# One weight load of 128 rows issued as seven loads of 8, 8, 8, 8, 8, 8 and 80 rows

## The chip, the core and the metric

The kernel runs on one core of a Trainium2 chip. The metric is the device time of one execution in microseconds (us), as the median over runs; lower is better. The trace of one profiled execution shows five engines: PE (matrix multiplication, with PEld for its weight loads), DVE (vector work), ACT (activations and copies), POOL (small vector work) and SP, which does nothing in this kernel but issue DMA transfers. The transfers themselves run on the core's 16 DMA engines.

## What is computed

Three layers in a row, all in float32: a windowed attention, a soft mixture of eight experts, and a gated feed-forward layer.

```
scores = scale * np.matmul(q, k.transpose(0, 1, 3, 2))      # masked to a window, softmax, then @ v
...
slot_input = slot_input.reshape(E, S_per_e, D)              # E = 8 experts, 4 slots each
for e in range(E):
    h = np.maximum(slot_input[e] @ w1[e], 0.0)
    slot_out[e] = h @ w2[e]
...
h = x @ w_in
g = h * (1.0 / (1.0 + np.exp(-h)))
return (g @ w_out).astype(np.float32)
```

The change concerns how one sixteenth of the experts' second weight matrix, `w2`, is brought from memory.

## The kernel before

The attention runs over 16 pairs of heads until about 96 us. While it runs, SP already brings in the experts' weights: `w1` in 16 pieces and `w2` in 16 pieces, each a tile of 128 rows by 2048 numbers (1 MB). Then PE runs the expert layer: L1.0 to L1.15 multiply by the pieces of `w1`, and L2.0 to L2.15 by the pieces of `w2`, one group of matmuls for each piece. In the listing `l1(i)` and `l2(i)` are these groups, `load_w1(i)` and `load_w2(i)` the loads. After the last of them come the weights of the third layer, `w_in` (tiles `wi0`, `wi1`, ...) and `w_out` (tiles `wo0`, ...). They arrive as 64-bit numbers and DVE converts them with three operations each (`conv`, lines 634, 636 and 638: the groups `cvi` for `w_in` and `cvo` for `w_out`). `wi0` and `wo0` come as two halves of 512 KB each. From about 134 us on PE multiplies without a break until the end.

What is issued when:

- All loads are issued by SP from one list, in one fixed order: ... `w2.7`, `w2.8`, `w2.9` to `w2.13`, the two halves of `wo0`, the first half of `wi0`, `w2.14`, `w2.15` in three parts, the second half of `wi0`, `wi1`, `wo1` and so on. SP handles one issue after the other; what waits there holds back all behind it.
- From `w2.8` on a piece of `w2` is loaded into a place that held a piece of `w1`, so its issue waits until PE has multiplied by that piece: `w2.8` waits for L1.1, `w2.9` for L1.2, up to `w2.13` for L1.6. The halves of `wo0` go where `w1.14` was, so they wait for L1.14.
- The framework gives each load, in the order of issue, one of eight semaphores in turn (`DMAHW0` to `DMAHW7` in the order listings). A load is issued only when the load that had the same semaphore before, eight places earlier in the list, has landed in full. At most eight loads are under way.
- The order on the engines in this part of the program is written out by hand (`LATER`, from line 1270); on DVE the conversions come in the order `hr1` (line 550, the last step of L1), `cvo` of the first half of `wo0`, and so on, to the conversion of the second half of `wi0`, after which PE makes its first operand of the third layer.

Two lines say how the operation that the change touches is put in the list:

```
   577	    for i in range(16):
   580	            op(f"lw2.{i}", "SP", 2.46, d, lambda i=i: load_w2(i))
```

Of the kernel before, what the change touches and what calls it, by code (L numbers as in the profile page):

```python
# [23 lines left out]
DFF = 2048  # L24
NT = B * S
EPS = 1e-9
XW = 129
JH = 6
CBANK = ((2, 1), (5, 1), (4, 6), (5, 1))
# [3 lines left out]
def fused_kernel(ctx: ExitStack, tc: tile.TileContext, a: dict):  # L33
    nc = tc.nc
    pe, act, dve, pool, sp = nc.tensor, nc.scalar, nc.vector, nc.gpsimd, nc.sync
# [20 lines left out]
    gmx = cp.tile([128, 1], F32, name="gmx")  # L56
    acc = cp.tile([128, XW], F32, name="acc")
    mrun = cp.tile([128, 2], F32, name="mrun")
# [16 lines left out]
    def new(place, key, dt=F32):  # L75
        tiles[key] = cp.tile([128, SIZE[place]], dt, tag=place, name=f"{place}_{key}")
        return tiles[key]

    def reg(key, off, n):
        return tiles[key][:, off:off + n]  # L80
# [4 lines left out]
    def mm(out, lhsT, rhs, start, stop):  # L85
        pe.matmul(out, lhsT=lhsT, rhs=rhs, start=start, stop=stop, skip_group_check=True)  # L86
# [11 lines left out]
    def op(name, eng, cost, deps, fn):  # L98
        kind = name.rstrip("0123456789.")
        if kind in INORDER and kind in last:  # L100
            deps = deps + [last[kind]]
        last[kind] = name
        ops[name] = (eng, cost, [d for d in deps if d], fn)
# [47 lines left out]
    def xreg(n):  # L151
        return reg("xb", (n % 5) * 5 * XW, 5 * XW).rearrange("p (t c) -> p t c", t=5)

# [88 lines left out]
    def recip(n, j0=0, j1=NJ):  # L242
        r, rows = n % 2, slice(j0 // 3, j1 // 3)
        dve.tensor_scalar(out=sume[:, r, rows], in0=sums[:, r, j0:j1].rearrange("p (a b) -> p a b", b=3), scalar1=EPS, scalar2=None, op0=ALU.add)  # L244
        dve.reciprocal(out=rinv[:, r, j0:j1].rearrange("p (a b) -> p a b", b=3), in_=sume[:, r, rows])  # L245
# [155 lines left out]
    def dc(b):  # L401
        for t in range(5):
            m = rows(t)
            for g in range(4):
                mm(mb[32 * g:32 * g + 32, 192:192 + XW], le[0:m, t, :], xreg(4 * b + g)[0:m, t, :], t == 0, t == 4)

# [4 lines left out]
    def ca4(b):  # L411
        dve.tensor_reduce(out=csm, in_=cn, axis=AXX, op=ALU.add)
        dve.tensor_scalar(out=csm, in0=csm, scalar1=EPS, scalar2=None, op0=ALU.add)  # L413
        dve.reciprocal(out=csm, in_=csm)
# [31 lines left out]
    for b in range(B):  # L446
# [4 lines left out]
            out=gmx, in_=lb[:, 0:160], axis=AXX, op=ALU.max))  # L451
# [12 lines left out]
        if b:  # L464
            op(f"dwe{b}", "ACT", .3, [f"dw{b}", f"ds{pb}"], lambda b=b: act.activation(out=wgt, in_=mrun, func=ACTF.Exp, bias=t4[:, 1:2]))
            op(f"dacc{b}", "DVE", .55, [f"dwe{b}"], lambda b=b: dacc(b))
            op(f"ds{b}", "DVE", .35, [f"dc{b}", f"dacc{b}"], lambda b=b: dve.scalar_tensor_tensor(
                out=acc, in0=mb[:, 192:192 + XW], scalar=wgt[:, 1:2], in1=acc, op0=ALU.mult, op1=ALU.add))
        else:
            op(f"ds{b}", "DVE", .2, [f"dc{b}"], lambda b=b: dve.tensor_copy(acc, mb[:, 192:192 + XW]))  # L470
        op(f"caa{b}", "DVE", .32, las + [f"cab{pb}" if b else f"pt{NPAIR-4}.3", "sie" if b == B - 1 else None],
# [29 lines left out]
    def fz():  # L501
        dve.tensor_scalar(out=t4[:, 2:3], in0=acc[:, 128:129], scalar1=EPS, scalar2=None, op0=ALU.add)
        dve.reciprocal(out=t4[:, 2:3], in_=t4[:, 2:3])
# [29 lines left out]

    def load_w2(i, g0=0, g1=4):
        t = new(W2S[i], f"w2.{i}") if g0 == 0 else tiles[f"w2.{i}"]
        sp.dma_start(out=t[:, 512 * g0:512 * g1], in_=a["w2"][i, :, 512 * g0:512 * g1])

    def l1(i):
        h, e = divmod(i, 8)
# [37 lines left out]
    for i in range(16):  # L577
        d = free2.get(W2S[i], []) + ([f"L1.{i-7}"] if i >= 8 else [])
        if i < 15:
            op(f"lw2.{i}", "SP", 2.46, d, lambda i=i: load_w2(i))  # L580
        else:
            for k, n in enumerate(("lw2.15", "lw2b", "lw2c")):
                op(n, "SP", .00482 * (W2C[k + 1] - W2C[k]), d, lambda k=k: load_w2(15, W2C[k] // 128, W2C[k + 1] // 128))
        d = [f"lw2.{max(i, L2W)}", f"hr{i//8}", f"te{N1}", f"L2.{i-1}" if i else None]
        if i < 15:
            op(f"L2.{i}", "PE", .86, d, lambda i=i: l2(i))
        else:
            op("L2a", "PE", .46, d, lambda: l2(15, 0))
            op("L2b", "PE", .24, ["L2a", "lw2b"], lambda: l2(15, 1))
            op("L2.15", "PE", .34, ["L2b", "lw2c"], lambda: l2(15, 2))  # L590
# [243 lines left out]
    for f in (0, 1, *range(2, 16, 2)):  # L834
        i = f // 2
# [213 lines left out]
    for c in range(NC):  # L1049
# [17 lines left out]
        for j in range(4):  # L1067
            r = lambda b: [f"cs{c}.{'ABCE'.index(b)}.{i}" for i in (2 * j, 2 * j + 1)]
# [5 lines left out]
        for g, p in enumerate(SEQ):  # L1074
            for j in range(4):
# [3 lines left out]
                r = lambda b: [f"cs{c}.{'ABCE'.index(b)}.{i}" for i in (2 * j, 2 * j + 1)]  # L1079
# [4 lines left out]
            for i in range(8):  # L1084
# [3 lines left out]
                for y in (6, 7) if i > 5 else (i,):  # L1088
                    d += [f"sh{c}.{p}.{y//2}", f"sl{c}.{p}.{y//2}"]
                    t = 3 if k == 4 else k  # L1090
# [431 lines left out]
```

## Time and profile before

| what | us |
|---|---|
| median of 3 runs | 344.35 (343.3 to 344.42) |
| the profiled execution | 343.64 |
| its span, first to last instruction | 341.5 |
| PE busy | 329.4 (96% of the span) |
| DVE busy | 263.3 (77%) |
| ACT busy | 221.9 (65%) |
| DMA: bytes moved | 70.03 MB, mean 205 GB/s |

The profiled execution is 2.1 us longer than its span: what lies before the first and behind the last instruction. Its slices of time (40 of 8.5 us each) show the DMA engines full and moving 400 to 420 GB/s from 8 us to 136 us, and nearly idle after 150 us. The granted TensorE clock is full speed in every slice. The rows below come from six views: the chain of waits (the work that ended last, followed back), the busy time by stretch, the issues in order of time on SP, the list of transfers with the time from issue to landing, the waits of SP's queue, and the instructions of DVE and PE in order of time.

### The profile page before, as it was taken

The page shows a single profiled execution, that of the slowest core. Times are in us where ns is not written, and L with a number is a line of the kernel's source. Part 1 is how long each engine was busy: PE and PEld are TensorE (multiplying, and loading weights), DVE is VectorE, ACT ScalarE, POOL GpSimd, SP SyncE. Part 2 cuts the span into 40 slices and gives each one's busy share as a digit, 9 for nine tenths or more (in the row PEclk, how much of TensorE's full clock was granted, in tenths as well). Part 3 has the DMA queues.
Part 4 walks back from the last instruction along what each step waited for, and adds up shares of the span by engine and source line. Part 5 has one row for each costly group of instructions (what it writes and reads, how often), then busy time and mean ns, then how long its engine had stood idle before and what let it go on. Part 6 is the DMA issues. An engine that isn't in the chain of part 4 may idle for free.

```text
span 341.5 us, 8179 instructions
## 1 busy us (share of the span) xinstructions
PE 329.4 (96%) x3221; PEld 272.1 (80%) x3232; DVE 263.3 (77%) x479; ACT 221.9 (65%) x639; POOL 74.6 (22%) x121
## 2 busy tenths in 40 slices
PE   7998999999899999999999999999999999999995
PEld 3687877777633337788888888999999999999995
DVE  5777877689660099999999997989994654999573
ACT  3599989797430125778496999996467666645540
POOL 6987978675260000000000000000000000000000
PEclk9999999999999999999999999999999999999999
DMA  7999999999999999818390000110200011000004
GB/s 259 405 405 406 403 401 407 416 404 415 416 405 423 416 411 419 349 58 322 125 356 15 0 0 2 55 68 2 77 3 0 0 71 69 3 23 23 2 22 147
DMA packets 17893, 70.03 MB, mean 205 GB/s; under 512 B 1984, under 2 KB 4288, under 8 KB 12096
## 3 DMA queue, kind: packets, MB, share of 16 engines
q1 hardware_dynamic: 17856, 69.53, 51.9%
q8 instruction: 25, 0.41, 0.5%
q14 instruction: 12, 0.10, 0.1%
HBM read 64.80 MB, written 4.72 MB: 204 GB/s over the span
## 4 chain that ended last, share of the span: by engine, by line
PE 83%; DMA 8%; DVE 3%; ACT 2%; POOL 1%; issue 1%; DVEq 0%; ACTq 0%; POOLq 0%
PE ps L86 80%; DMA w_w2.13_1760<-in_w 5%; PE ps L312 3%; DMA w_wi<-in_w_in 3%; ACT rt_px L232 1%; DMA rs_raw<-in_q 1%; POOL rv_v L1138 1%; ACT rt_px L301 1%; POOL rb_a L180 0%; PE ps L434 0%; POOL ra_a L180 0%; ACT x_xb L315 0%; DVE stats L227 0%; DVE csm L413 0%; DVE spaced L244 0%
## 5 line engine op out<-in xcount | busy, mean ns | idle before, releaser
L1083 DVE TENSOR_TENSOR rt_stl<-w_raww,rs_sth 128x768 fp32r<-128x768 f32 (+1 forms) x52 | 42.2, 830 | 18.2 <-ACT rs_sth L1081 17.9
L86 PE MATMUL ps<-w_ws,x_gz 128*128 128x512 f32 x216 | 53.6, 393 | 0.0
L86 PE MATMUL ps<-rs_sth,w_ws 128*128 128x384 f32 x192 | 53.1, 334 | 0.0
L1081 ACT CAST rs_sth<-w_raww 128x768 fp32r<-128x768 f32 (+1 forms) x52 | 37.8, 738 | 22.3 <-PE ps L86 16.6
L232 ACT ACTIVATE rt_px<-ps,spaced 128x64 f32<-128x64 f32 x144 | 43.5, 332 | 10.2 <-DVE spaced L228 8.5
L86 PEld LDWEIGHTS ps<-w_ws,x_gz 128*128 128x128 f32 x216 | 40.0, 188 | 7.7 <-issue 0.4
L86 PEld LDWEIGHTS ps<-rs_sth,w_ws 128*128 128x128 f32 x192 | 35.1, 188 | 0.0
L232 ACT ACTIVATION_READ_ACCUMULATOR rt_px<-ps,spaced 128x1 f32 x144 | 32.3, 225 | 0.0
L86 PE MATMUL ps<-rt_stl,w_ws 128*128 128x384 f32 x96 | 32.1, 334 | 0.0
L86 PE MATMUL ps<-ct_ct,rv_astk 128*128 128x384 f32 x96 | 27.3, 338 | 0.0
L1066 ACT ACTIVATE w_raww<-ps 128x384 f32<-128x384 f32 x48 | 22.0, 493 | 7.1 <-PE ps L86 7.0
L249 POOL TENSOR_TENSOR rt_px<-rt_px,stats 128x576 f32<-128x576 f32 (+2 forms) x17 | 18.6, 1093 | 8.2 <-DVE stats L245 3.4
L86 PEld LDWEIGHTS ps<-ct_ct,rv_astk 128*128 128x128 f32 x96 | 17.6, 188 | 2.4 <-issue 0.4
L86 PEld LDWEIGHTS ps<-rt_stl,w_ws 128*128 128x128 f32 x96 | 18.0, 188 | 0.0
L896 ACT ACTIVATE x_gz<-ps 128x768 fp32r<-128x768 f32 (+3 forms) x18 | 13.3, 740 | 4.8 <-PE ps L86 4.7
L899 DVE TENSOR_TENSOR x_gz<-rt_gtm,x_gz 128x768 fp32r<-128x768 f32 (+3 forms) x18 | 15.5, 864 | 1.0 <-ACT rt_gtm L889 0.9
L1081 ACT CAST rs_sth<-x_rawx 128x768 fp32r<-128x768 f32 x12 | 10.0, 837 | 9.6 <-PE ps L86 6.3
L889 ACT ACTIVATE rt_gtm<-ps 128x768 f32<-128x768 f32 (+3 forms) x18 | 13.2, 742 | 3.8 <-PE ps L86 3.6
L86 PEld LDWEIGHTS ps<-ra_a,rv_v 128*64 128x64 f32 x320 | 13.3, 137 | 2.8 <-issue 1.1
L86 PE MATMUL ps<-ra_a,rv_v 128*64 128x96 f32 (+2 forms) x320 | 14.9, 241 | 0.4 <-DVE ra_a L263 0.3
L1083 DVE TENSOR_TENSOR rt_stl<-x_rawx,rs_sth 128x768 fp32r<-128x768 f32 x12 | 11.5, 954 | 4.7 <-ACT rs_sth L1081 4.6
L315 ACT COPY x_xb<-ps 128x640 f32<-128x640 f32 x16 | 11.3, 708 | 5.7 <-PE ps L312 3.5
(298 smaller groups left out, 772.2 us busy)
## 6 DMA issues: line engine op xcount, KB each, us to landing
w_wi<-in_w_in SPq DMA_DIRECT2D x7, 1024.0 KB, 7.1
rs_wo<-in_w_out SPq DMA_DIRECT2D x4, 1024.0 KB, 5.8
rk_k<-in_k SPq DMA_DIRECT2D x12, 288.0 KB, 7.6
w_wo<-in_w_out SPq DMA_DIRECT2D x3, 1024.0 KB, 4.7
rs_raw<-in_v SPq DMA_DIRECT2D x9, 288.0 KB, 9.4
rs_raw<-in_q SPq DMA_DIRECT2D x8, 288.0 KB, 6.5
w_more<-in_q SPq DMA_DIRECT2D x8, 288.0 KB, 9.4
w_more<-in_v SPq DMA_DIRECT2D x6, 288.0 KB, 8.0
```

The source lines that it names most:

```text
L86: pe.matmul(out, lhsT=lhsT, rhs=rhs, start=start, stop=stop, skip_group_check=True)
L232: act.activation(out=preg(n)[:, j, :], in_=sj(n, j), func=ACTF.Exp, scale=D ** -0.5, bias=nmx[:, r, j // 3, j % 3:j % 3 + 1], accum_out=su ...
L249: pool.tensor_tensor(out=p, in0=p, in1=rinv[:, n % 2, j0:j1].rearrange("p (j o) -> p j o", o=1).to_broadcast([128, j1 - j0, 64]), op=ALU.mult)
L301: act.copy(out=x, in_=src)
L312: pe.transpose(ps[0:m, c:c + 128], x[:, 128 * t:128 * t + m], ident)
L315: act.copy(out=xreg(n)[:, :, 0:128], in_=ps[:, TC:TC + 640].rearrange("p (t c) -> p t c", c=128))
L889: act.activation(out=cols(gt(f), x), in_=hbs(x), func=ACTF.Silu)
L896: act.activation(out=cols(gbuf(f, 0), x), in_=hbs(x), func=ACTF.Silu)
L899: dve.tensor_tensor(out=gsl(gbuf(f, 1), x), in0=gsl(gt(f), x), in1=gsl(gbuf(f, 0), x), op=ALU.subtract)
L1066: op(f"cs{x}", "ACT", .385, [f"ch{x}", *d], lambda c=c, b=b, i=i, s=s: act.activation(out=at(c, b, i), in_=bank[6 + s][:, 0:TW], func=ACTF ...
L1081: op(f"sh{x}", "ACT", cost(c, PRODS[p][0], j, .42, .74), [*src, old, "cvo14" if o < 0 else None], lambda c=c, p=p, j=j: both(c, p, j, 0, l ...
L1083: lambda c=c, p=p, j=j: both(c, p, j, 1, lambda x, h, l: dve.tensor_tensor(out=l, in0=x, in1=h, op=ALU.subtract)))
```

## The change

`load_w2` issues one transfer for a piece of `w2`, rows 0 to 128. With the change, piece 8 alone is issued as seven transfers: rows 0 to 8, 8 to 16, and so on to 40 to 48, and then rows 48 to 128. All seven write into the same tile, from the same place in memory, and together they move the same 1 MB.

```
+EIGHTS = [(r, r + 8) for r in range(0, 48, 8)] + [(48, 128)]
...
     def load_w2(i, g0=0, g1=4):
         t = new(W2S[i], f"w2.{i}") if g0 == 0 else tiles[f"w2.{i}"]
-        sp.dma_start(out=t[:, 512 * g0:512 * g1], in_=a["w2"][i, :, 512 * g0:512 * g1])
+        for r0, r1 in EIGHTS if i == 8 else ((0, 128),):
+            sp.dma_start(out=t[r0:r1, 512 * g0:512 * g1], in_=a["w2"][i, r0:r1, 512 * g0:512 * g1])
```

No instruction of PE, DVE, ACT or POOL changes its place. On SP the list grows by six rows, and the semaphores in brackets move with it. In the listings `w_w2.8_1683` is the tile of piece 8, the brackets hold what the issue waits for, and `PE_49` is PE's own semaphore. SP around piece 8, before:

```order
L536 DMA rv_w2.6_1634<-in_w 128x2048 [waits DMAHW0_49,Activation_49,Pool_49]
L536 DMA rt_w2.7_1661<-in_w 128x2048 [waits DMAHW1_49,PE_49,Activation_49]
L536 DMA w_w2.8_1683<-in_w 128x2048 [waits DMAHW2_49,PE_49]
L536 DMA w_w2.9_1704<-in_w 128x2048 [waits DMAHW3_49,PE_49]
L536 DMA w_w2.10_1720<-in_w 128x2048 [waits DMAHW4_49,PE_49]
L536 DMA w_w2.11_1734<-in_w 128x2048 [waits DMAHW5_49,PE_49]
```

SP at the same place, after:

```order
L538 DMA rv_w2.6_1634<-in_w 128x2048 [waits DMAHW0_49,Activation_49,Pool_49]
L538 DMA rt_w2.7_1661<-in_w 128x2048 [waits DMAHW1_49,PE_49,Activation_49]
L538 DMA w_w2.8_1683<-in_w 8x2048 [waits DMAHW2_49,PE_49]
L538 DMA w_w2.8_1683<-in_w 8x2048 [waits DMAHW3_49]
L538 DMA w_w2.8_1683<-in_w 8x2048 [waits DMAHW4_49]
L538 DMA w_w2.8_1683<-in_w 8x2048 [waits DMAHW5_49]
L538 DMA w_w2.8_1683<-in_w 8x2048 [waits DMAHW6_49]
L538 DMA w_w2.8_1683<-in_w 8x2048 [waits DMAHW7_49]
L538 DMA w_w2.8_1683<-in_w 80x2048 [waits DMAHW0_49]
L538 DMA w_w2.9_1710<-in_w 128x2048 [waits DMAHW1_49,PE_49]
L538 DMA w_w2.10_1726<-in_w 128x2048 [waits DMAHW2_49,PE_49]
L538 DMA w_w2.11_1740<-in_w 128x2048 [waits DMAHW3_49,PE_49]
```

Piece 8 now takes the seven semaphores 2 to 7 and 0. Piece 9 shared semaphore 3 with `w2.1`; it now shares semaphore 1 with `w2.7`, which stands eight places ahead of it. The 80-row load shares semaphore 0 with `w2.6`, and pieces 10 to 13 share theirs with four of the 8-row loads.

## Rows read from the trace of the kernel before

**Rows 1.** The chain of waits: start us, length us, what.
```profile
102.94 15.57 DMA w_w2.13_1760<-in_w
...
118.52 10.18 DMA w_wi<-in_w_in
...
128.72 0.43 DVE w_wif L634
...
134.21 203.75 PE ps L86 x1167
```

**Rows 2.** Stretches: length, busy PE, PEld, DVE, ACT, POOL; clock, DMA, GB/s.
```profile
103.00:118.50 15.50, 15.50 (x140) 5.18 (x132) 0.29 (x1) 1.77 (x4) 0.00 (x0) 1.00 1.00 416
```

**Rows 3.** Issues on SP in order of time: start us, length us, line, transfer.
```profile
12.54 0.33 SPq L530 DMA_DIRECT2D w_w1.1_319<-in_w  x1
13.30 0.33 SPq L530 DMA_DIRECT2D w_w1.2_371<-in_w  x1
...
91.81 0.33 SPq L536 DMA_DIRECT2D rt_w2.7_1661<-in_w  x1
98.65 0.33 SPq L536 DMA_DIRECT2D w_w2.8_1683<-in_w  x1
99.50 0.33 SPq L536 DMA_DIRECT2D w_w2.9_1704<-in_w  x1
...
109.80 0.81 SPq L625 DMA_DIRECT2D w_wo<-in_w_out  x2
...
126.17 0.43 SPq L620 DMA_DIRECT2D w_wi<-in_w_in  x1
```

**Rows 4.** Transfers issued at 12.54, 13.30, 91.81, 99.50, 109.80, 126.17, 156.93: us to landing.
```profile
w_w1.1_319<-in_w SPq DMA_DIRECT2D x1, 1024.0 KB, 10.1
...
w_w1.2_371<-in_w SPq DMA_DIRECT2D x1, 1024.0 KB, 12.8
...
rt_w2.7_1661<-in_w SPq DMA_DIRECT2D x1, 1024.0 KB, 11.8
...
w_w2.9_1704<-in_w SPq DMA_DIRECT2D x1, 1024.0 KB, 9.0
...
w_wo<-in_w_out SPq DMA_DIRECT2D x1, 512.0 KB, 10.0
...
w_wi<-in_w_in SPq DMA_DIRECT2D x1, 1024.0 KB, 14.9
...
rs_wo<-in_w_out SPq DMA_DIRECT2D x1, 1024.0 KB, 4.7
```

**Rows 5.** Waits of SP's queue, 98 to 120: us, times, longest.
```profile
SPq L536 <- DMA w_w2.11_1734<-in_w: 1.5, 1, 1.5
```

**Rows 6.** Stretches at the end of the full DMA queue; last: DMA share, GB/s.
```profile
137.00:138.00 1.00, 1.00 (x6) 0.78 (x5) 1.00 (x3) 0.88 (x2) 0.00 (x0) 1.00 0.95 393
...
138.50:139.50 1.00, 1.00 (x6) 0.57 (x5) 1.00 (x3) 0.98 (x2) 0.00 (x0) 1.00 0.59 246
```

**Rows 7.** Instruction fetches, 21-24 us, then 116-119 us: packets, MB, share of 16 engines.
```profile
q8 instruction: 1, 0.02, 2.3%
...
q8 instruction: 1, 0.02, 2.2%
```

**Rows 8.** DVE in order of time: start, length, line, [idle before, releaser].
```profile
119.41 0.29 DVE L550 TENSOR_SCALAR x_sip<-ps 128x128 f32<-128x128 f32 x1 [8.32 <-PE ps L86]
119.80 0.43 DVE L634 TENSOR_SCALAR w_wt<-w_wo 128x512 uint32<-128x512 uint32 x1
...
128.25 0.42 DVE L723 TENSOR_TENSOR w_wt<-w_wt 128x256 f32<-128x256 f32 x1
128.72 0.43 DVE L634 TENSOR_SCALAR w_wif<-w_wi 128x512 uint32<-128x512 uint32 x1
```

**Rows 9.** PE in order of time, the same columns.
```profile
120.54 1.04 PE L86 MATMUL ps<-w_w2.8_1683,x_sip 128*32 128x512 f32 x8
...
130.87 1.08 PE L86 MATMUL ps<-w_wif,lg 128*32 128x128 f32 x32 [0.38 <-DVE w_wif L638]
```

## The prediction, written before the changed kernel ran

> **What bounds the kernel now.** I read the chain of waits first [rows 1]. From 134.21 us PE multiplies for 203.75 us without a break to the end, so whatever moves the start of that stage moves the end by as much. Ahead of it the chain goes through two transfers: `w2.13`, which lands at 118.51, and the second half of `wi0`, issued then and landed at 128.70, which DVE starts to convert at 128.72. So the stretch from 103 to 134 looks bound by DMA. Two other views correct this [rows 2, 8]: PE is busy for all of 103.0 to 118.5, and DVE's last step of L1 (119.41 to 119.70) waits for PE, not for a load. DVE then converts the first half of `wo0` at 119.80, the moment it lands (109.80 + 10.0) [rows 3, 4], and works on until 128.67, so that the conversion at 128.72 comes right behind other DVE work as well [rows 8]. PE waits for the end of that conversion at 130.87 [rows 9]. Two paths therefore meet within 0.1 us: the stream of loads, and PE and DVE's own work. Loads that land earlier gain 0.1 us at most, since DVE is not free before 119.70; loads that land later cost all of their delay, from 119.80 on.
>
> **The change, part by part.**
>
> *Six more issues.* SP needs 0.81 us for two issues without a wait [rows 3], 0.41 each and some 0.43 to 0.47 with the step between. The seven parts of piece 8 go out from 98.65 to about 101.4. Nothing there waits: the semaphores that they share belong to `w2.0` to `w2.6`, and the last of these lands at about 101.1, one load of 2.5 us ahead of `w2.7`. Piece 8 itself is needed by PE at 120.54 [rows 9], so its own delay costs nothing.
>
> *Piece 9 waits for `w2.7`.* This is the new wait. SP does hold a load until the one eight places ahead has landed [rows 5]. `w2.7` lands at 91.81 + 11.8 = 103.6 [rows 3, 4]. Piece 9 was issued at 99.50 and now goes out at 103.6, 4.1 us later; queued behind it are pieces 10 to 13 and all further loads. Pieces 10 to 13 wait for 8-row loads that have landed by then, and follow within 2 us. The halves of `wo0` still wait for PE until 109.80.
>
> *What the DMA engines do meanwhile.* At 103.6 only piece 8 is left to them. A load that finds the engines empty lands 4.7 us after its issue (the last row of [rows 4]), and one in a full stream takes 2.5 us: from `w2.9` (99.50 + 9.0 = 108.5) to `w2.13` (118.51) there are four steps in 10.0 us. So an issue needs about 2.2 us until its data flow. The 80 rows, issued at 101.4, flow at 103.6 and take 80/128 x 2.5 = 1.6 us, to about 105.2; piece 9 flows from 105.8. The engines are empty for about 0.6 us. Piece 9 lands at 103.6 + 4.7 = 108.3, where it landed at 108.5: **-0.2 us** for the engine that comes last.
>
> *What this takes from the other engines.* That small number hides the main thing. Before, the 16 engines were not level. Where the full stream ends, their share falls from 0.95 to 0.59 by 138.5 to 139.5 [rows 6], while the load issued at 126.17 lands only at 141.1 [rows 3, 4]: some seven of them had run out more than 1.5 us ahead of the last. A landing waits for the last engine alone, so these had a lead in which a delay of their own did not show. With the change all of them wait for piece 9, and the lead is gone.
>
> *The fetch at 117 us.* PE's instructions come over the same engines. One fetch of 16 KB lies in 116 to 119 and takes 2.2% of 16 engines in 3 us, 1.06 us of one engine [rows 7]. Before it was not seen: `w2.13` lands 2.5 us behind its forerunner and the half of `wo0` 1.3 us behind that. A fetch can be seen, though: `w1.1` lands at 22.6 and `w1.2` at 26.1, 3.5 us for a step of 2.5, with a fetch of the same size between [rows 3, 4, 7]. So it costs a landing from 0 (it strikes an engine with a lead) to about 1.4 (1.06 and a row of 8 KB in flight, 2.5/8 = 0.31). With the lead gone I take **1.2**: it lies near the 1.0 and the 1.06, and 1.0 is the least that the engine struck lost, as it need not have been the last before.
>
> *Sum.* -0.2 + 1.2 = +1.0 us at the landing of the first half of `wo0`, of the other halves and of `w2.15` behind it. DVE starts at 120.8 instead of 119.80, the stage at 134.21 begins 1.0 later, and nothing behind it takes the delay back, as PE has no gap there. The profiled execution of 343.64 lies 0.2% under the median of the runs; by its own time the sum gives 344.64, by the median 344.35 + 1.0 = 345.35, which I take. The ends: -0.2 leaves DVE's own 0.1, so 344.25; 1.4 for the fetch gives 345.55.
>
> [...] No row here tells how an 8-row load is spread. [...]
>
> **The rivals.**
>
> *The fetch stays hidden.* The engine that the fetch strikes at 117 may have kept enough lead, or the engines may be level by less than I think. Then only the -0.2 is left, DVE lets 0.1 of it through: 344.25. For it: before, this very fetch was hidden. Against: no engine can have had data of piece 9 before 105.8. [...]
>
> *The rows are taken off the engines that come last (not slower).* If the six small loads run on engines that are ahead, each row moved saves 0.31 us on the last ones, three rows 0.9 us, as long as piece 9 follows without a gap, that is if its data flow within 1.3 us of its issue rather than 2.2. The landings come 0.9 earlier and a fetch eats that up; DVE, not free before 119.70, lets 0.1 through: 344.25 again, and never under 344.0 by way of the loads alone.
>
> *The small loads are slow.* A fetch holds an engine for 1.06 us where two rows of data take 0.62 [rows 7], so a small transfer may cost 0.44 us beyond its data. Six in a row would be 6 x 0.75 = 4.5 us instead of 1.9, from 100.9 to 105.4, and with the five rows of the 80 to 107.0, 1.2 us past the 105.8 at which piece 9 would flow. From there each us costs one: 345.35 + 1.2 = 346.55.
>
> **How the numbers follow.** The forecast (345.35, between 344.9 and 345.8) gets 0.60, the hidden fetch 0.20, the moved rows 0.12, the slow loads 0.08. About what a measurement of this kernel can tell from no change is 0.3%, here 1.03 us, and the forecast lies just at it: of its 0.60 I put 0.37 above and 0.23 below. Slower is then 0.37 + 0.08 = 0.45; faster gets 0.05 of the moved rows' 0.12, for a gain that the rows do not show; the rest, 0.50, is within 0.3%. The range goes from 344.1, a little under the two rivals at 344.25, to 346.1, which leaves out the slow loads and the gain.
>
> **What would show it.** In the changed kernel's trace: piece 9 issued at 103.6 and landed near 108.3; a dip of the DMA share near 105; the first half of `wo0` landed near 120.8 and its conversion starting then; the long PE stage from about 135.2. The forecast is wrong if piece 9 goes out before 103, if `wo0` lands by 119.8, if DVE starts it at 119.8 or if the long stage makes up for a late start.

## The result, and the profile after

The changed kernel takes 348.28 us (median of 6 runs, 347.29 to 350.43) against 343.71 us for the kernel before (343.0 to 344.42). The ratio is 1.0143, 95% interval 1.0107 to 1.018: **slower by 4.6 us**, where +1.0 was forecast and 346.1 was the top of the range. The profiled execution took 348.01 us, 4.4 more than the profiled one of before.

The chain of waits of the changed kernel (start us, length us, what), to be laid beside [rows 1]:

```profile
90.93 15.10 DMA rt_w2.7_1661<-in_w
106.09 5.56 DMA w_w2.9_1710<-in_w
111.67 17.09 DMA w_w2.14_1825<-in_w
128.80 3.43 PE ps L87 x32
...
139.13 12.75 PE ps L87 x67
151.91 190.49 PE ps L87 x1097
```

The new wait is on it, as forecast: `w2.9` goes out when `w2.7` has landed, and `w2.14` when `w2.9` has. But `w2.7` lands at 106.03 and not at 103.6. The issues on SP (start, length, line, transfer, count), to be laid beside [rows 3]:

```profile
97.77 4.16 SPq L538 DMA_DIRECT2D w_w2.8_1683<-in_w  x7
106.09 0.36 SPq L538 DMA_DIRECT2D w_w2.9_1710<-in_w  x1
106.56 0.37 SPq L538 DMA_DIRECT2D w_w2.10_1726<-in_w  x1
```

The transfers from issue to landing (count, KB each, us), as [rows 4] shows them for before:

```profile
rt_w2.7_1661<-in_w SPq DMA_DIRECT2D x1, 1024.0 KB, 15.1
w_w2.9_1710<-in_w SPq DMA_DIRECT2D x1, 1024.0 KB, 5.6
```

So `w2.9` lands at 106.09 + 5.6 = 111.7, 3.1 us later than before; 0.2 us earlier was forecast. The busy time by stretch shows where `w2.7` lost its time (last two columns: share of the 16 DMA engines that was busy, and GB/s). The first row is the full stream as it was before too:

```profile
96.00:98.00 2.00, 2.00 (x24) 0.56 (x20) 1.70 (x4) 1.08 (x4) 1.60 (x2) 1.00 1.00 418
100.00:102.00 2.00, 2.00 (x24) 0.65 (x20) 0.68 (x3) 1.63 (x3) 0.45 (x1) 1.00 0.90 238
102.00:104.00 2.00, 2.00 (x24) 0.56 (x20) 0.00 (x0) 0.69 (x1) 0.00 (x0) 1.00 0.91 221
104.00:106.00 2.00, 2.00 (x24) 0.61 (x20) 0.00 (x0) 0.00 (x0) 0.00 (x0) 1.00 0.91 197
106.00:107.00 1.00, 1.00 (x16) 0.29 (x12) 0.00 (x0) 0.00 (x0) 0.00 (x0) 1.00 0.32 90
107.00:108.00 1.00, 1.00 (x16) 0.36 (x12) 0.00 (x0) 0.00 (x0) 0.00 (x0) 1.00 1.08 180
```

These are the rows to learn to read. From 100 to 106 the engines are busy for nine tenths of the time, and move about half of the full stream's 418 GB/s. They are hardly short of work: by these rows each byte takes 1.6 to 1.9 times as long (418 against 238/0.90, 221/0.91 and 197/0.91). In 106 to 107 many of them are short of work, but this is not the gap that the prediction spoke of, with piece 8 through and piece 9 not yet flowing. The 80 rows of piece 8, issued at 101.61, land 7.8 us later, at 109.4, where the prediction had them through at 105.2; from 107 to 108 the engines are busy again, at 180 GB/s:

```profile
w_w2.8_1683<-in_w SPq DMA_DIRECT2D x1, 640.0 KB, 7.8
```

SP's waits between 98 and 125 (us in all, times, longest) show what comes next:

```profile
SPq L538 <- DMA rt_w2.7_1661<-in_w: 4.1, 1, 4.1
SPq L538 <- DMA w_w2.12_1750<-in_w: 2.9, 1, 2.9
...
SPq L538 <- DMA w_w2.11_1740<-in_w: 2.2, 1, 2.2
SPq L538 <- DMA w_w2.10_1726<-in_w: 2.1, 1, 2.1
SPq L538 <- DMA rv_w2.6_1634<-in_w: 1.8, 1, 1.8
```

The waits for `w2.10` to `w2.12` are one step of the stream each. The third is longer by 0.7 to 0.8 us. The profile has one instruction fetch of PE between 115.5 and 117 (3.9% of the 16 engines in these 1.5 us, or 0.94 us of one engine), just ahead of it; that the fetch, which was hidden before, is the cause is the prediction's mechanism, and fits. DVE (start, length, line, operation, in brackets the idle time before it and what ended it), to be laid beside [rows 8]:

```profile
118.53 0.29 DVE L552 TENSOR_SCALAR x_sip<-ps 128x128 f32<-128x128 f32 x1 [8.32 <-PE ps L87]
123.83 0.43 DVE L636 TENSOR_SCALAR w_wt<-w_wo 128x512 uint32<-128x512 uint32 x1 [5.01 <-DMA w_wo<-in_w_out]
...
132.67 0.43 DVE L636 TENSOR_SCALAR w_wif<-w_wi 128x512 uint32<-128x512 uint32 x1
```

The conversion of `wo0` starts at 123.83 instead of 119.80, 4.0 us later, and that of the second half of `wi0` at 132.67 instead of 128.72, 3.95 later. Nothing behind takes it back. PE, which had no pause here before, now has one:

```profile
128.80 1.72 PE L87 MATMUL ps<-w_w2.14_1825,x_sip 128*32 128x512 f32 x8 [3.80 <-DMA w_w2.14_1825<-in_w]
```

and behind it the granted clock (the third column from the right) falls to half, 0.50 of full speed from 130 to 132 us:

```profile
128.00:130.00 2.00, 1.20 (x8) 0.16 (x8) 2.00 (x4) 0.24 (x1) 0.00 (x0) 0.77 1.01 392
130.00:132.00 2.00, 2.00 (x28) 1.08 (x24) 1.88 (x4) 0.38 (x1) 0.00 (x0) 0.50 1.06 437
132.00:134.00 2.00, 2.00 (x24) 1.52 (x22) 1.76 (x5) 1.29 (x5) 0.00 (x0) 0.88 1.04 434
```

### The profile page after: what moved, and what is told of

The parts are those of the page before. It is cut to its first block, busy times and chain, and to the rows that moved or that the text cites. A ratio compares the mean times of both kernels' runs of the same rounds, so it can differ in the third digit from the quotient of the medians.

```text
span 345.9 us, 8190 instructions
## 1 busy us (share of the span) xinstructions
PE 331.5 (96%) x3221; PEld 272.9 (79%) x3232; DVE 263.2 (76%) x479; ACT 221.7 (64%) x639; POOL 74.4 (22%) x121
## 4 chain that ended last, share of the span: by engine, by line
PE 74%; DMA 13%; DVE 4%; ACT 3%; POOL 2%; SPq 1%; issue 1%; POOLq 0%; ACTq 0%
PE ps L87 71%; DMA w_w2.14_1825<-in_w 5%; DMA rt_w2.7_1661<-in_w 4%; PE ps L313 2%; DMA w_more<-in_q 2%; DMA w_w2.9_1710<-in_w 2%; ACT rt_px L233 2%; POOL rt_px L250 1%; ACT rt_px L302 1%; POOL rv_v L198 1%; ACT rt_px L300 0%; DVE ra_a L261 0%; DVE ra_a L259 0%; ACT x_xb L316 0%; PE ps L435 0%
## 5 line engine op out<-in xcount | busy, mean ns | idle before, releaser
L1085 DVE TENSOR_TENSOR rt_stl<-x_rawx,rs_sth 128x768 fp32r<-128x768 f32 x12 | 11.5, 954 | 4.7 <-ACT rs_sth L1083 4.6
L87 PE MATMUL ps<-rb_a,rv_v 128*64 128x96 f32 (+2 forms) x320 | 14.5, 241 | 0.1
```

The lines of the kernel that those rows point to most:

```text
L1085: lambda c=c, p=p, j=j: both(c, p, j, 1, lambda x, h, l: dve.tensor_tensor(out=l, in0=x, in1=h, op=ALU.subtract)))
```

## The experiments

Three theories of the 4.6 us went in. **P**: it matters which rows of the tile the DMA engines write at the same time; engines that write neighbouring rows hold each other up. **G**: the new wait of `w2.9` alone. **S**: many small loads are slow, wherever they write. (Each ratio is against the kernel before as timed beside that run.)

### Seven loads without neighbouring rows

Seven loads with the same semaphores and the same wait, but every load has all 128 rows:

```
-EIGHTS = [(r, r + 8) for r in range(0, 48, 8)] + [(48, 128)]
+PARTS = [(c, c + 256) for c in range(0, 1536, 256)] + [(1536, 2048)]
...
+            sp.dma_start(out=t[:, c0:c1], in_=a["w2"][i, :, c0:c1])
```

> Piece 8 in seven loads as in the changed kernel, but cut along the columns: six of 128 rows by 256 columns, one of 128 rows by 512. The semaphores, and with them the wait of piece 9 for w2.7, are those of the changed kernel. Theory P (neighbouring rows: eight DMA engines writing to eight neighbouring rows hold each other up, so that a row takes 0.44 to 1.3 us instead of 0.31) expects full speed here: w2.7 landed at 102.7 to 103.6 (106.0 in the changed kernel), piece 9 landed near 108.3, the first half of wo0 converted from 120.0 to 120.8, and 343.7 to 344.8 us in all. Theory G (the new wait alone) expects the time of the changed kernel, about 348, since the wait is the same. Theory S (many small loads are slow, wherever they write) expects w2.7 near 106 and about 348 as well.

Measured: 345.44 us against 343.50, ratio 1.0059 (1.0041 to 1.0077). The transfers:

```profile
rt_w2.7_1661<-in_w SPq DMA_DIRECT2D x1, 1024.0 KB, 12.6
w_w2.9_1710<-in_w SPq DMA_DIRECT2D x1, 1024.0 KB, 5.2
```

`w2.7`, issued at 90.91, lands at 103.5, as the prediction had it for the changed kernel; `w2.9` goes out at 103.62 and lands at 108.8; DVE starts at 121.04. This is almost the kernel that I had forecast. Its wait is the changed kernel's and its loads are as many (six of 128 KB and one of 256 KB, where that one has six of 64 KB and one of 640 KB), and it loses 1.9 us where that one loses 4.6: neither the wait nor the number of loads carries the whole loss. What is over the expected 344.8 comes up again in the last run.

The same with whole rows that stand apart: four loads of every fourth row of 0 to 31, two of every second row of 96 to 127, and rows 32 to 95.

```
+PARTS = [slice(k, 32, 4) for k in range(4)] + [slice(96, 128, 2), slice(97, 128, 2)] + [slice(32, 96)]
```

> Piece 8 in seven loads of whole rows, same semaphores and same wait as in the changed kernel, but the rows of a small load stand apart: four loads of 8 rows take every fourth row of 0 to 31, two loads of 16 rows take every second row of 96 to 127, and the last takes rows 32 to 95. Theory P expects near full speed: w2.7 landed by 104.2, piece 9 landed at 108.3 to 109.5, DVE at the first half of wo0 from 120.0 to 121.7, 343.7 to 345.6 us. Theory G and theory S expect the changed kernel's 348, with w2.7 at 106 by S. [...]

Measured: 347.11 us, ratio 1.011 (1.0069 to 1.0152). Theory P missed by 1.5 us. `w2.7` landed at 91.26 + 14.1 = 105.4, and the engines were busy for only 0.81 of 100 to 104 us. The run also has two loads of 16 rows within rows 96 to 127 and an issue every 0.7 us, both of which the expectation had left out; it doesn't tell them apart, so this miss stays open, and the next pairs are cleaner.

### Two large loads, by rows and by columns

Two loads of 512 KB, so no small load and no new wait, once by rows (the first line) and once by columns (the second):

```
+PARTS = [slice(0, 64), slice(64, 128)]
...
+PARTS = [(0, 1024), (1024, 2048)]
```

> Piece 8 in two loads of 64 rows, 0 to 63 and 64 to 127: no small load, and no wait that binds, since piece 9 shares its semaphore with w2.4, landed at 96.1. Theory P expects that two engines meet at each place and a row takes up to 0.62 us: piece 9 landed 0.6 to 2.5 us later than the 108.5 of before, DVE at the first half of wo0 from 120.4 to 122.3, 344.3 to 346.2 us. Theories G and S expect the time of before, 343.4 to 344.0. [...]

> The control of the halves: piece 8 in two loads of 128 rows by 1024 columns. The same number of loads, the same bytes, the same semaphores. All theories expect the time of before, 343.4 to 344.0, and piece 9 landed at 108.5; if it comes out slower, the second issue and not the place of the rows is what costs.

Measured: by rows 348.25 us, ratio 1.0147 (1.0115 to 1.018); by columns 343.57 us, ratio 1.0002 (0.9993 to 1.0011). Halving one load by rows costs as much as the whole change, without its wait and without a small load. The stretch from 100 to 104 us, by rows:

```profile
100.00:104.00 4.00, 4.00 (x44) 1.21 (x40) 0.68 (x3) 2.23 (x4) 0.89 (x3) 1.00 1.03 225
```

and by columns:

```profile
100.00:104.00 4.00, 4.00 (x44) 1.17 (x36) 0.68 (x3) 2.50 (x4) 0.46 (x1) 1.00 1.02 406
```

The engines are fully busy in both, and move 225 and 406 GB/s. Piece 9 lands at 99.72 + 12.8 = 112.5, 4.0 us late. Theory P had allowed 2.5, and 346.2 us in all, since it counted piece 8 alone and not what piece 8 does to the tail of `w2.7` (landed at 91.59 + 14.1 = 105.7, against 91.12 + 12.9 = 104.0 by columns). That two engines meet at one place, so that a row takes up to 0.62 us, was P's assumption here and in the pair of 64 rows below; no run shows where the engines meet.

### Two pairs that differ in the rows

Six loads of the same sizes in the same order, with four small ones over rows 0 to 31, of neighbouring rows (the first line) or of every fourth row (the second):

```
+PARTS = [slice(r, r + 8) for r in range(0, 32, 8)] + [slice(32, 96), slice(96, 128)]
...
+PARTS = [slice(k, 32, 4) for k in range(4)] + [slice(32, 96), slice(96, 128)]
```

> Piece 8 in six loads: four of 8 neighbouring rows (0 to 31), one of rows 32 to 95, one of 96 to 127. Piece 9 then shares its semaphore with w2.6 and waits for nothing new. It is one half of a pair with the next run. Theory P expects rows of the small loads at 0.44 us and more as in the changed kernel, w2.7 landed 0.7 to 2.5 us late (104.3 to 106.1), and 344.5 to 347.0 us in all. Theory G expects 343.5 to 344.0, since the wait is gone. Theory S expects a loss, and the same one in both halves of the pair.

> The other half of the pair: the same six loads of the same sizes with the same semaphores, but the four small loads take every fourth row of 0 to 31 each. Theory P expects most of the loss of the other half to be gone: w2.7 landed by 104.2, piece 9 landed at least 0.7 us ahead of the other half's, 343.5 to 345.0 us. [...] Theories G and S expect no difference between the halves.

Measured: neighbours 349.06 us, ratio 1.0149 (1.0114 to 1.0185), above P's 347.0; every fourth row 346.57 us, ratio 1.0083 (1.0069 to 1.0097). From issue to landing, neighbours:

```profile
rt_w2.7_1661<-in_w SPq DMA_DIRECT2D x1, 1024.0 KB, 14.7
w_w2.9_1709<-in_w SPq DMA_DIRECT2D x1, 1024.0 KB, 10.5
```

and every fourth row:

```profile
rt_w2.7_1661<-in_w SPq DMA_DIRECT2D x1, 1024.0 KB, 11.5
w_w2.9_1709<-in_w SPq DMA_DIRECT2D x1, 1024.0 KB, 6.7
```

`w2.7` lands at 91.04 + 14.7 = 105.7 and at 92.12 + 11.5 = 103.6: the tail of the load ahead is held up where the rows of the small loads are neighbours, and not where they are not. The second half still costs 2.9 us, more than P's 345.0. Its engines were busy for only 0.68 of 100 to 104 us, against 1.03 in the first half. SP's issues of piece 8, neighbours and then every fourth row:

```profile
97.87 2.64 SPq L538 DMA_DIRECT2D w_w2.8_1683<-in_w  x6
98.96 4.06 SPq L538 DMA_DIRECT2D w_w2.8_1683<-in_w  x6
```

The same six issues took SP 2.64 us and 4.06 us (piece 9 went out at 102.10 and 103.14), and the four small loads bring 64 KB each, so in the second half the engines run short of work. So this pair differs in more than the rows: the slower issues came with the spread rows, and what small loads cost without them it does not show. A part of the 2.5 us between the two is the clock as well; in the one execution of each with a mean granted clock of 1.0 they took 347.05 and 345.94 us.

The clean pair has one load of 64 rows, from the same rows of memory, with only the place in the tile changed. The other half of piece 8 is left out and set to zero by POOL. For rows 0 to 63 (for the other, `LOADED` is rows 32 to 95):

```
+LOADED = slice(0, 64)
...
+            sp.dma_start(out=t[LOADED, 0:2048], in_=a["w2"][i, 0:64])
```

> Only half of piece 8 is loaded, 64 rows in one load, written to rows 0 to 63; POOL sets the other 64 rows to zero, so the product of piece 8 is not the reference's. One of a second pair: the same source rows, bytes, number of loads and DMA engines as in the next run. Theory P expects two engines to meet at each place here: a row takes up to 0.62 us, w2.7 lands later than in the next run, and piece 9 0.6 to 3 us later than in the next run; in time 343.5 to 346. Theories G and S expect no difference between the two.

> The other of the second pair: the same 64 rows from memory, written to rows 32 to 95; POOL sets the other 64 rows to zero, so the product of piece 8 is not the reference's. Theory P expects rows at 0.31 us, w2.7 landed as before near 103.6, piece 9 about 1.2 us ahead of the 108.5 of before (half a load less), and 343.4 to 344.0 us, since DVE is not free earlier. [...]

Measured: rows 0 to 63 348.55 us, ratio 1.0127 (1.009 to 1.0164); rows 32 to 95 342.71 us, ratio 0.9975 (0.9961 to 0.9989). P had the order right and allowed too little between the two: 343.5 to 346 and 343.4 to 344.0. The stretch from 100 to 104 us for rows 0 to 63:

```profile
100.00:104.00 4.00, 4.00 (x40) 1.17 (x36) 1.35 (x5) 1.10 (x2) 2.75 (x4) 1.00 1.03 240
```

and for rows 32 to 95:

```profile
100.00:104.00 4.00, 4.00 (x44) 1.21 (x40) 1.33 (x5) 1.01 (x2) 2.82 (x4) 1.00 1.00 408
```

This settles it: 5.8 us between two kernels that read the same memory with the same single load, with POOL busy for as long (2.75 and 2.82 us of the stretch). It is not the reading, nor the size or number of loads, nor a wait, but the rows of the tile that are written together. Being neighbours is not the point, since both are blocks of 64 neighbouring rows; which rows they are decides. In the profiled executions 3.5 us of this is the landing: DVE starts on the first half of `wo0` at 122.42 and at 118.97. The rest lies behind it, where PE paused for 2.45 us for `w2.14` in the first kernel and the granted clock then stood at 0.50 from 130 to 136; that kernel's one execution with a mean clock of 1.0 took 345.8 us.

The halves agree with this: with rows 0 to 63 and 64 to 127 loaded apart the engines moved 225 GB/s in 100 to 104 us, and 240 with rows 0 to 63 alone, both with the tail of another load in the stretch, against 408 with rows 32 to 95. Why the one set of rows is written more slowly than the other, no run shows, nor how the engines shared the writing of the 8-row loads in the changed kernel.

### The clock behind PE's pause

The changed kernel with PE's pause filled by 12 matmuls that nobody reads, and the changed kernel once more beside it:

```
+        for c in range(GAPMM if i == 13 else 0):
+            mm(bank[2][:, 0:128], hsb[:, 0:128], hsb[:, 128:256], True, True)
```

> The changed kernel with 12 more matmuls of 128 by 128 behind L2.13 on PE, whose result nobody reads; they fill the 3.8 us in which PE waits for w2.14. Loads and waits are those of the changed kernel, so the first half of wo0 is converted from about 123.8 again. Theory C (what the changed kernel loses behind its late landings, about 0.6 us in the median and up to 2.5 in single executions, is the granted clock at half speed after PE's wait) expects the clock at 1.00 all through 124 to 136 us, and 347.0 to 347.7 us with little spread. Theory N (the clock costs nothing, the rest is the landings) expects the changed kernel's time, 348.0 to 348.6, with its spread.

> The changed kernel itself once more, on the same chip as the one with the filled wait, to be compared with it: 347.9 to 348.7 us, w2.7 landed near 106.0, the granted clock at about half for 2 us or more between 128 and 136 us.

Measured: filled 347.55 us (347.21 to 347.97), ratio 1.0112 (1.0099 to 1.0125); unchanged 349.20 us (347.36 to 350.5), ratio 1.0158 (1.0125 to 1.019), above the expected 348.7. Behind the filled pause:

```profile
128.00:130.00 2.00, 1.77 (x18) 0.72 (x20) 2.00 (x4) 0.56 (x1) 0.00 (x0) 1.00 1.05 401
130.00:132.00 2.00, 1.75 (x26) 0.59 (x18) 1.85 (x5) 0.43 (x3) 0.00 (x0) 1.00 1.06 432
```

and behind the pause as it was:

```profile
130.00:132.00 2.00, 2.00 (x24) 0.80 (x24) 1.92 (x4) 0.62 (x1) 0.00 (x0) 0.50 1.05 423
132.00:134.00 2.00, 2.00 (x22) 1.30 (x14) 1.82 (x6) 1.14 (x4) 0.00 (x0) 0.74 1.03 426
```

The clock is 1.6 us of the median here, from 4 and 6 executions whose intervals just touch, and it is the spread: single executions of the changed kernel with a mean granted clock of 1.0 took 347.3 to 347.5 us, those with 0.985 some 350.

The run of the unchanged kernel shows one thing more. Its loads of pieces 7 and 9, from issue to landing:

```profile
rt_w2.7_1661<-in_w SPq DMA_DIRECT2D x1, 1024.0 KB, 14.3
w_w2.9_1710<-in_w SPq DMA_DIRECT2D x1, 1024.0 KB, 7.4
```

`w2.7` lands at 91.16 + 14.3 = 105.5, half a microsecond earlier than in the first profile, and `w2.9`, issued at 105.50, only at 112.9; in the filled run it takes 6.9 us. How the delay divides between the two pieces changes from execution to execution.

### Seven column loads with the pause filled

The seven column loads with four more matmuls in PE's pause of 1.05 us:

```
+GAPMM = 4
 PARTS = [(c, c + 256) for c in range(0, 1536, 256)] + [(1536, 2048)]
```

> The seven loads cut along the columns (six of 256 columns, one of 512), with four more matmuls of 128 by 128 behind L2.13 on PE, whose result nobody reads, in the 1.05 us in which PE waits for w2.14. This leaves of the change the new wait alone: rows as spread as before, and PE without the pause behind which the clock fell. If the wait costs what the late start of DVE showed in the seven column loads (121.04 instead of 119.80, the fetch in it), the time is 343.7 + 0.6 to 1.3 = 344.3 to 345.0 us; if the 1.9 us of the seven column loads was the wait's own and not the clock's, it stays at 345.3 to 345.6.

Measured: 345.43 us against 343.91, ratio 1.0046 (1.0033 to 1.006), the granted clock at 1.00 from 124 to 136 us in the profile. Of the two outcomes named before, the second came: the time is that of the seven column loads without the filling, 345.44, although in that run's profile the granted clock had stood at 0.58 and 0.56 from 130 to 134, behind the pause of 1.05 us. So the seven loads and their order of issue cost 1.5 us here without that fall of the clock. How much of it is the wait is not shown: in this execution SP was busy with the seven issues from 99.25 to 103.63 us, and `w2.9` followed at 103.73 with no wait for `w2.7` on SP's list, where the first column run had one of 2.2 us. SP's waits show one part of the 1.5 us:

```profile
SPq L626 <- DMA w_w2.13_1766<-in_w: 3.1, 1, 3.1
SPq L539 <- DMA w_w2.12_1750<-in_w: 2.1, 1, 2.1
```

The step with the fetch is 1.0 us longer than the one before it. The other part is the landing of `w2.9`, 5.4 us after an issue at 103.73, so at 109.2 instead of 108.5.

## Why the prediction was wrong, step by step

**What bounds the kernel.** Right as to losses: the lateness of the first half of `wo0`, 4.0 us, came through to the end in full. Wrong as to gains: I allowed 0.1 us, and held 344.0 for a floor. The load of 64 rows on rows 32 to 95 gained 1.0 us against the run beside it. DVE's last step of L1 began at 118.76 there, and in the traces of all these kernels anywhere from 118.51 to 120.02, so the 119.41 of the one trace I had of before was that execution's and no floor.

**Six more issues.** Nearly right: the seven go out from 97.77 to 101.9, the last of them after a wait of 1.8 us for `w2.6`, which I had seen as landed. The 80 rows went out at 101.61, 0.2 us later than I took.

**Piece 9 waits for `w2.7`.** The wait was right, its end was not. I took `w2.7`'s landing of 103.6 from the trace of before, as though loads behind it in the queue could not touch it. **This is the step that failed.** It landed at 106.03, 2.4 us late, and at 105.0 and 105.5 in the two later traces with the same loads. That piece 8's rows held up its tail follows from the pair of 64-row loads, where it landed at 106.5 and 103.4 by the choice of rows alone; for the 8-row loads it is the same sign in the profile and no clean pair.

**The engines between.** That the 80 rows take 80/128 x 2.5 us failed for the same reason: a load's time was not its bytes over the full stream's rate, here or in the halves. They landed at 109.4 instead of about 105.2, so piece 9 did not find empty engines, and the 4.7 us were too short: 5.6 in the changed kernel, 6.9 and 7.4 in the two later traces with its loads, 5.2 and 5.4 in the column runs. The term of -0.2 was +3.1 in the changed kernel, and +0.3 and +0.7 in the two column runs.

**The fetch.** The mechanism fits, the size was a little high: 1.2 was taken, and 0.7 to 0.8 showed in the changed kernel, 1.0 in the column runs. In the two later executions with the changed kernel's loads SP's waits lengthened by 0.3 us and by nothing, which would fit a fetch that strikes an engine with a lead; no view here names the engine.

**The sum.** In the changed kernel's trace, 2.4 at `w2.7`, 0.9 at `w2.9` (5.6 instead of 4.7) and the forecast's own -0.2 make the +3.1 at `w2.9`; with the 0.7 to 0.8 of the fetch they make the 4.0 at the first half of `wo0`, and 0.4 came behind it, where the clock fell. So the sign was right, but of the 4.6 us only the fetch came by the path that I had named. With seven loads cut by columns the forecast came nearer: +1.0 was forecast, with ends of -0.1 and +1.2, and +1.5 was measured (345.43 against 343.91), beyond that end and within the range. With PE's pause filled in both, the changed kernel lost 3.8 us (347.55 against 343.75), so the cut by rows added 2.3 to that of the columns; how much of this is the crowding of the rows and how much the smaller loads is not shown. The clock added 0.7 (348.28) to 1.6 us (349.20).

**The rivals.** "The small loads are slow" had the right sign and the right place for the wrong reason: it priced an overhead per transfer at 0.44 us, 1.2 us in all, where two loads of 512 KB lose 4.7 us with no small one among them. It was given 0.08. No run shows how a load of 8 rows is spread over the engines; the three rows of the moved rows (8 of 128 for each of 16 engines, less 5 of 80) and the "six in a row" of the slow loads rested on assumptions. What the changed kernel showed in their place is engines busy for 0.90 to 0.91 of 100 to 106 us at 197 to 238 GB/s. The two rivals at 344.25 are out, and the range left out the time because every case in it took the rate of the engines as given.

**The clock** was in no case. A pause of PE had been seen as no more than its length; the prediction said that PE was busy from 103.0 to 118.5 and did not ask what a pause of 3.8 us behind that does.

## What to carry to other kernels

Before a load is cut by rows, ask which rows are written at the same moment: cutting in two by columns was free here (343.57 us against 343.50), and cutting by rows at 64 cost 4.7 us. Half of the delay showed at the load ahead in the queue, which landed 1.7 us later than with the columns, where piece 9 landed 3.4 us later. A transfer share near 1.0 with half the GB/s is the sign of it in a profile (here 1.03 with 225 GB/s by rows, 1.02 with 406 by columns): the engines are busy, not idle. When a late load makes a busy PE pause, price the clock behind the pause too, in the spread of the runs (up to 3.1 us here) as well as in the median (1.6 us, 349.20 against 347.55).

## What the hardware showed that I had not expected

- With one load of 64 rows from the same memory in the stream, the engines moved 240 GB/s in 100 to 104 us when it was written to rows 0 to 63, and 408 GB/s when to rows 32 to 95; the busy share was 1.03 and 1.00.
- A load can be held up by one that was issued behind it: `w2.7` landed at 105.0 to 106.5 with loads of 8 neighbouring rows or of rows 0 to 63 behind it, and at 103.4 to 104.0 with column loads, four loads of every fourth row, or rows 32 to 95 behind it. In the run with two loads of 16 rows it landed at 105.4, which stays open.
- After a pause of 3.8 us the granted clock stood at 0.50 for 2 us and more in the profiled executions, and executions of the same kernel differed by up to 3 us with it (347.36 us at a mean clock of 1.0, 350.5 at 0.985). Behind a pause of 1.05 us, in the seven column loads, it stood at 0.58 and 0.56 in 130 to 134 us; with that pause filled it stayed at 1.00 from 124 to 136 us.
